# Two placements in a fused attention and feed-forward kernel: the scale of the second weight, and the planes of the last head pair of batch 0

## The chip, the cores and the metric

The kernel runs on one core of one Trainium2 chip. The metric is the time of one execution in device microseconds (us); of several runs the median is given. A change of more than 0.3% (about 3.1 us) is what a measurement of this kernel can tell from no change.

## What is computed

Eight batches of eight heads attend over 512 local tokens and 32 global ones (head size 64). A global query sees all 544 keys, a local query the global keys and the local keys within 32 positions. The result, 4352 rows of 512, goes through a feed-forward block.

```python
s_ll = np.where(np.abs(pos[:, None] - pos[None, :]) <= 32, s_ll, -1e9)
a_l = sm(np.concatenate([s_lg, s_ll], axis=-1))          # softmax
out_l = np.matmul(a_l, np.concatenate([v_g, v_l], axis=2))
x = attn_out.transpose(0, 2, 1, 3).reshape(B * S, H * D)
h = x @ w_in                                             # 512 -> 2048
g = h * np.cos(h)
return g @ w_out                                         # 2048 -> 512
```

## The kernel before

All matmuls are done in fp16 with each operand held as a high plane and a low plane (value minus high), so each product is three matmuls. Planes need scales, powers of two taken from the largest absolute value.

**Weights.** `w_in` and `w_out` come as raw 64-bit words. For `w_out`, `w_out_max` (L401) loads each of 16 row blocks and reduces it to its largest value; `w_out_done` (L428) joins the 16 results, spreads the maximum over the partitions with one matmul into a PSUM tile `pm_wo` (`spread_max`, L183), reads it back and makes the scale `wsc`. Only then can `w_out_piece` (L418) decode the 16 blocks. For each, ACT scales the words (`y_wo`, L237), DVE makes the low bits (L263, L266, which need no scale) and joins them (L268), ACT rounds to the high plane (L281) and POOL subtracts for the low plane (L231, two instructions). Blocks 8 to 15 are loaded again into a ring of two buffers (L244), so that a load waits until an earlier block is decoded.

**Attention.** It goes by pairs of heads, four pairs to a batch. For each pair come scores (L606, L607), row minima (L623), exponentials (L446), probability planes in four query tiles (`sc_d`, L672), their transposes (`sc_e`, L707), the product with v (`av_a`, `acc`, L729) and the planes `xh`, `xl` of the feed-forward's input (`av_b`, L766). In batch 0 the transposes are done by TensorE: eight of 128x128 into one PSUM tile `tr`, copied to `pt` by DVE for tiles 0 and 2 and by ACT for tiles 1 and 3 (L715). The table `PLS` says for batch 0 how each tile of each pair makes its planes:

- 1: per head, ACT writes the high plane straight from the exponentials (L702), DVE the low plane (L705)
- 2: per head, DVE writes the high plane (L704), DVE the low plane (L705)
- 3 and 4: the exponentials are normalized in place by POOL (3, L685) or ACT (4, L688); ACT rounds (L693), POOL subtracts per head (L695)

**Feed-forward.** A chunk is 256 tokens. `m1_a` (L908) makes the first product into PSUM tiles `ph`, `m1_b` to `m1_d` the cosine, `m2_a` (L975 to L977) the second product, which needs the decoded blocks of `w_out`.

**The order.** Work is written into numbered slots, and in a slot into phases (PA0 first, PJ last); walking through slots and phases gives the program's order. Tiles of one tag share buffers, and in the program's order each new tile waits for a buffer that an earlier one gives back. The tag `ph` has three PSUM buffers, for `tr`, for `acc` of the last two pairs of batch 0, for `pm_wo` and for the `ph` tiles. A second number, the priority, says which ready instruction an engine's order takes first; `at(slot, phase, f, ..., pr=(slot, phase))` sets it apart from the place in the program, and without `pr` both are the same. A planner then fixes each engine's queue, and on the chip each queue runs in that order.

Pair p of batch 0 starts at slot u = -21 + p; its planes are in slot u + 5, its transposes in slot u + 6 (phase PA2), its `acc` in slot u + 7. So the transposes of pair 2 stand in slot -13 and those of pair 3 in slot -12. The first two `ph` tiles are opened in slot -5; `w_out_done` stands in slot -4, phase PJ.

Of the kernel before, what the change touches and what calls it, by code (L numbers as in the profile page):

```python
# [65 lines left out]
GFB = 3  # L66
GFW = 3
UW = 1
PLS = [[3, 4, 3, 4], [3, 4, 3, 4], [3, 4, 3, 4], [1, 2, 1, 4]]
DEFN = [0, 0]  # L70
TPE = [1, 1, 1, 1]
TPV = [1, 0, 1, 0]
# [37 lines left out]
WO = -13  # L110
WOS = 2
WOL = -5
WOD = -4
GWM = 0
U1 = 2
SP1 = 2
# [21 lines left out]
def body(tc, qk, v, wi, wo, mask, out):  # L138
# [5 lines left out]
    with ExitStack() as ctx:  # L144
# [527 lines left out]
        def sc_d(b, p, i):  # L672
# [3 lines left out]
            w = WIN[i][1]  # L676
            pl = PLS[p][i] if b == 0 else (PL0, PL1, PL)[min(b, 2)]
            if b < 2 and DEFN[b]:
# [327 lines left out]
        def at(slot, phase, f, *a, pr=None):  # L1006
            e = (phase, len(ev[slot]), f, a)
            ev[slot].append(e)
            pr = (slot, phase) if pr is None else pr if isinstance(pr, tuple) else (pr, phase)
            rank[slot, e[1]] = pr + (slot, e[1])  # L1010
# [75 lines left out]
                at(WE + k, PJ, w_in_load, k + 4, pr=W0 + k)  # L1086
        at(WE + 7, PA, w_in_done, pr=(W0 + 7 - WM, PH2))
        for k in range(16):
            at(WO + k // WOS, PI, w_out_max, k)
        for k in range(8):  # L1090
            at(WOL, PJ, w_out_load, k)
        at(WOD, PJ, w_out_done)
        for k in range(16):
            at(k // 2 + PO, WOPH, w_out_piece, k)
        at(LV1, PJ, load_v, 1)
# [113 lines left out]
```

## Time and profile before

| | |
|---|---|
| median of 3 runs (lowest to highest) | 1033.6 us (1032.02 to 1034.86) |
| the profiled execution: its own time | 1034.44 us |
| its span in the trace | 1032.6 us |
| busy: PE, ACT, DVE, POOL | 87%, 70%, 69%, 45% of the span |
| mean granted TensorE clock | 0.954 |

The span runs from the first to the last recorded instruction; the execution's own time holds 1.8 us more. Busy shares are means over the whole span, and the stages differ: up to about 245 us the weights are prepared and batches 0 and 1 go through attention, after that the steady loop over chunks runs.

### The profile page before, as it was taken

The numbers are of one execution on the slowest core, as the hardware profiler recorded it, in microseconds if no ns is written. First come the engines' busy times: TensorE is split into PE (matmuls) and PEld (weight loads), VectorE is DVE, ScalarE is ACT, GpSimd is POOL, SyncE is SP. The second block draws the span as 40 slices with busy tenths as digits, with TensorE's granted clock in tenths as the row PEclk, the third lists the DMA queues.
The fourth block names the chain that finished last, engine by engine and source line by source line (L and its number), as shares of the span: only waits on it lengthen the run. The fifth ranks groups of instructions, "written<-read, shape, count | busy, mean of one in ns | idle before, by whom it ended". The sixth has DMA issues, their size and how long they took to land.

```text
span 1032.6 us, 21117 instructions
## 1 busy us (share of the span) xinstructions
PE 893.3 (87%) x7947; PEld 609.2 (59%) x7947; DVE 710.7 (69%) x1811; ACT 717.9 (70%) x1468; POOL 461.8 (45%) x494
## 2 busy tenths in 40 slices
PE   1245878769999999899899999999989999999996
PEld 0134645444666766666666666666666667766663
DVE  4999786897477777867777777868777766433231
ACT  5788798785577776877687768777777876544342
POOL 3696477984233333333334324343333343534442
PEclk9996979788999999999999999999989999999998
DMA  9796145775254464454645354545536452100000
GB/s 361 269 303 246 15 142 142 181 164 139 70 103 111 103 157 108 99 115 97 147 93 119 91 145 93 122 91 153 111 81 109 107 88 61 34 21 22 1 21 21
DMA packets 165822, 120.19 MB, mean 116 GB/s; under 512 B 143064, under 2 KB 143064, under 8 KB 163672
## 3 DMA queue, kind: packets, MB, share of 16 engines
q1 hardware_dynamic: 165720, 118.85, 46.3%
q8 instruction: 62, 1.02, 0.4%
q14 instruction: 40, 0.33, 0.1%
HBM read 56.00 MB, written 8.91 MB: 63 GB/s over the span
## 4 chain that ended last, share of the span: by engine, by line
PE 33%; DVE 28%; ACT 15%; DMA 11%; POOL 5%; issue 5%; SPq 1%; ACTq 0%; DVEq 0%; POOLq 0%
PE ph L919 13%; DMA qkr<-qk 7%; PE po L975 5%; PE po L976 5%; PE po L977 5%; DVE planes L705 4%; DVE t L623 4%; DVE u L942 3%; ACT L446 3%; ACT planes L702 3%; ACT t L446 3%; DMA vr<-v 2%; DVE kl L538 2%; POOL w L954 2%; DVE qm L497 2%
## 5 line engine op out<-in xcount | busy, mean ns | idle before, releaser
L919 PE MATMUL ph<-xh,wi_h 128*128 128x256 f16 x1024 | 281.9, 276 | 10.0 <-DVE gf L956 9.8
L919 PE MATMUL ph<-xl,wi_h 128*128 128x256 f16 x1024 | 282.1, 275 | 0.0
L919 PE MATMUL ph<-xh,wi_l 128*128 128x256 f16 x1024 | 282.0, 275 | 0.0
L961 POOL TENSOR_TENSOR gl<-gf,gh 128x512 f16<-128x512 f32 x136 | 167.2, 1233 | 236.5 <-ACT gh L960 236.5
L954 POOL TENSOR_TENSOR w<-w 128x512 f32<-128x512 f32 x136 | 141.5, 1044 | 266.0 <-ACT w L446 266.0
L919 PEld LDWEIGHTS <-wi_h 128*128 128x128 f16 x2176 | 211.8, 99 | 52.3 <-issue 12.4
L975 PE MATMUL po<-wo_h,gh 128*128 128x512 f16 x544 | 206.5, 384 | 28.2 <-DVE o L983 17.1
L976 PE MATMUL po<-wo_l,gh 128*128 128x512 f16 x544 | 209.6, 385 | 10.6 <-POOL wo_l L231 10.6
L977 PE MATMUL po<-wo_h,gl 128*128 128x512 f16 x544 | 209.5, 386 | 0.0
L446 ACT ACTIVATE w<-u,ca 128x512 f32<-128x512 f32 x136 | 97.8, 721 | 109.9 <-DVE u L942 109.3
L942 DVE SCALAR_TENSOR_TENSOR u<-u,cm,ph 128x512 f32<-128x512 f32 x136 | 100.9, 742 | 97.3 <-ACT u L941 97.3
L446 ACT ACTIVATE t<-t,mn 128x192 f32<-128x192 f32 (+1 forms) x256 | 116.9, 458 | 49.3 <-DVE mn L623 48.9
L956 DVE SCALAR_TENSOR_TENSOR gf<-w,ph 128x512 f32<-128x512 f32 x136 | 92.6, 682 | 58.3 <-POOL w L954 58.1
L960 ACT CAST gh<-gf 128x512 f16<-128x512 f32 x136 | 83.1, 611 | 69.8 <-DVE gf L956 59.2
L919 PEld LDWEIGHTS <-wi_l 128*128 128x128 f16 x1088 | 107.5, 99 | 15.1 <-issue 1.4
L623 DVE CUSTOM_DVE_ANT_0 t<-ps,msk,al 128x192 f32<-128x192 f32 (+1 forms) x256 | 99.5, 426 | 11.7 <-PE ps L607 11.2
L941 ACT ACTIVATE u<-ph,cm 128x512 f32<-128x512 f32 x136 | 92.1, 678 | 21.4 <-PE ph L919 19.5
L977 PEld LDWEIGHTS <-gl 128*128 128x128 f16 x544 | 53.8, 99 | 75.5 <-issue 13.9
L705 DVE SCALAR_TENSOR_TENSOR planes<-t,sm,planes 128x224 f16<-128x224 f32 (+1 forms) x198 | 88.6, 496 | 10.7 <-ACT planes L702 10.7
L976 PEld LDWEIGHTS <-gh 128*128 128x128 f16 x544 | 53.7, 99 | 70.7 <-issue 22.7
L975 PEld LDWEIGHTS <-gh 128*128 128x128 f16 x544 | 53.1, 98 | 62.8 <-issue 14.5
L702 ACT ACTIVATE planes<-t,sm 128x192 f16<-128x192 f32 (+1 forms) x196 | 74.3, 453 | 0.0
(185 smaller groups left out, 1427.7 us busy)
## 6 DMA issues: line engine op xcount, KB each, us to landing
qkr<-qk SPq DMA_DIRECT2D x29, 608.0 KB, 4.8
vr<-v SPq DMA_DIRECT2D x8, 1280.0 KB, 7.7
kh<-qa SPq DMA_DIRECT2D x62, 152.0 KB, 2.6
out<-o SPq DMA_DIRECT2D x34, 256.0 KB, 2.7
raw_wm<-wo SPq DMA_DIRECT2D x16, 512.0 KB, 7.6
qa<-kl SPq DMA_DIRECT2D x31, 152.0 KB, 3.9
kl<-kl SPq DMA_DIRECT2D x31, 152.0 KB, 4.6
wo_h<-wi SPq DMA_DIRECT2D x4, 1024.0 KB, 6.7
```

The source lines that it names most:

```text
L446: ins = nc.scalar.activation(*a, **k).ins
L623: nc.vector.tensor_tensor_reduce(t[:, h], pt[:, h], msk[:, MOFF[i] : MOFF[i] + w], al, 3.0e38, ALU.add, ALU.min, mn[:, h : h + 1],)
L702: nc.scalar.activation(hi, t[:, h], AF.Identity, scale=r)
L705: nc.vector.scalar_tensor_tensor(lo, t[:, h], r, hi, op0=ALU.mult, op1=ALU.subtract)
L919: nc.tensor.matmul(ph[:, a], w[:, kc, f], x[:, kc, q], start=first and ip == 0, stop=last and ip == 2, skip_group_check=True,)
L942: nc.vector.scalar_tensor_tensor(u, u, m, ph, op0=ALU.subtract, op1=ALU.subtract)
L954: nc.gpsimd.tensor_tensor(w, w, w, op=ALU.mult)
L956: nc.vector.scalar_tensor_tensor(gf, w, 0.5, st.pop(("ph", c, j)).rearrange("p a b -> p (a b)"), op0=ALU.subtract, op1=ALU.mult,)
L961: nc.gpsimd.tensor_tensor(gl, gf, gh, op=ALU.subtract)
L975: nc.tensor.matmul(po[k], gh[:, q], wo_h[:, f], start=(f == 0), stop=False)
L976: nc.tensor.matmul(po[k], gh[:, q], wo_l[:, f], start=False, stop=False)
L977: nc.tensor.matmul(po[k], gl[:, q], wo_h[:, f], start=False, stop=(f == NJ - 1))
```

## The change

```diff
-PLS = [[3, 4, 3, 4], [3, 4, 3, 4], [3, 4, 3, 4], [1, 2, 1, 4]]
+PLS = [[3, 4, 3, 4], [3, 4, 3, 4], [3, 4, 3, 4], [1, 1, 1, 1]]
...
-WOD = -4
+WOE = -20
...
         for k in range(16):
-            at(WO + k // WOS, PI, w_out_max, k)
+            at(WOE + k // WOS, PJ, w_out_max, k, pr=(WO + k // WOS, PI))
...
-        at(WOD, PJ, w_out_done)
+        at(WOE + 7, PJ, w_out_done, pr=(WO + 7, PI))
```

With `WO = -13` and `WOS = 2` the 16 maxima keep their priorities (slots -13 to -6, phase PI) but stand in the program in slots -20 to -13. `w_out_done` stands in slot -13, phase PJ, instead of slot -4, phase PJ; its priority goes from slot -4, phase PJ, to slot -6, phase PI. Separately, tiles 1 and 3 of pair 3 of batch 0 make their planes in way 1 instead of ways 2 and 4.

## Rows read from the trace of the kernel before

**Rows 1.** The page: the shares of the chain that ended last.

```profile
PE 33%; DVE 28%; ACT 15%; DMA 11%; POOL 5%; issue 5%; SPq 1%; ACTq 0%; DVEq 0%; POOLq 0%
```

**Rows 2.** Windows: us; busy time (instructions) by engine; clock, DMA share, GB/s.

```profile
98.20:104.80 6.60, 4.66 (x66) 3.84 (x63) 5.98 (x18) 6.60 (x15) 0.00 (x0) 0.79 0.00 1
104.80:112.40 7.60, 6.97 (x138) 5.83 (x139) 2.12 (x8) 3.16 (x7) 1.06 (x2) 1.00 0.02 4
112.40:245.00 132.60, 99.40 (x898) 66.27 (x896) 109.54 (x278) 113.48 (x228) 101.58 (x135) 0.81 0.58 136
245.00:1032.60 787.60, 749.16 (x6583) 510.17 (x6581) 509.36 (x1270) 522.57 (x1075) 291.87 (x257) 0.98 0.41 91
```

**Rows 3.** Timeline of DVE: start, duration, operation; in brackets its wait and releaser.

```profile
96.10 0.68 DVE L288 TENSOR_REDUCE wos<-raw_wm 128x1 f32<-128x512 f32 x1
...
97.95 0.29 DVE L186 TENSOR_SCALAR d_wo<-ident,wm_o 128x128 bf16<-128x128 f32 x1
...
111.68 0.28 DVE L190 TENSOR_REDUCE r_wo<-pm_wo 128x1 f32<-128x128 f32 x1
```

**Rows 4.** Timeline of PE, 98 to 112 us.

```profile
98.68 0.42 PE L750 MATMUL acc<-pt,vh 128*64 128x128 f16 x4
...
101.09 1.17 PE L714 MATMUL tr<-ident,planes 128*128 128x128 f16 x16
...
111.36 0.23 PE L188 MATMUL pm_wo<-d_wo,ones 128*128 128x128 bf16 x1
```

**Rows 5.** Timeline of ACT, 100 to 113 us.

```profile
100.07 1.55 ACT L702 ACTIVATE planes<-t,sm 128x192 f16<-128x192 f32 x4
101.51 0.79 ACT L688 ACTIVATE t<-t,sm 128x192 f32<-128x192 f32 x2
...
104.31 0.52 ACT L693 CAST planes<-t 128x384 f16<-128x384 f32 x1
107.94 1.01 ACT L715 COPY pt<-tr 128x1024 f16<-128x1024 f16 x1 [3.12 <-PE tr L714]
...
110.96 0.74 ACT L561 ACTIVATE vh<-vr 128x640 bf16<-128x640 f32 x1 [0.63 <-PE gacc L855]
...
112.42 0.75 ACT L237 ACTIVATE y_wo<-wo_h,wsc 128x512 f32<-128x512 f32 x1
```

**Rows 6.** Timeline of DVE at the last pair of batch 0.

```profile
99.83 0.58 DVE L704 TENSOR_SCALAR planes<-t,sm 128x224 f16<-128x224 f32 x2
...
101.18 1.45 DVE L705 SCALAR_TENSOR_TENSOR planes<-t,sm,planes 128x192 f16<-128x192 f32 x4
...
110.37 0.75 DVE L776 SCALAR_TENSOR_TENSOR xl<-acc,xs,xh 128x512 f16<-128x512 f32 x1 [5.08 <-ACT xh L775]
```

**Rows 7.** Timeline of POOL, 100 to 117 us.

```profile
104.96 1.06 POOL L695 TENSOR_TENSOR planes<-t,planes 128x192 f16<-128x192 f32 x2 [7.43 <-ACT planes L693]
114.99 1.75 POOL L231 TENSOR_TENSOR wo_l<-y_wo,wo_h 128x256 f16<-128x256 f32 x2 [8.98 <-ACT wo_h L281]
```

**Rows 8.** Waits of PE, 112 to 245 us: total us, times, longest.

```profile
PE po L975 <- ACT wo_h L281: 11.1, 5, 5.3
PE po L976 <- POOL wo_l L231: 10.6, 4, 5.2
```

**Rows 9.** Timeline: one DVE operation alone and beside POOL, and POOL then.

```profile
83.17 0.45 DVE L266 TENSOR_SCALAR lo_wo<-wo_h 128x512 uint16<-128x512 uint16 x1
...
127.26 1.28 DVE L266 TENSOR_SCALAR lo_wo<-wo_h 128x512 uint16<-128x512 uint16 x1
```

**Rows 10.** Timeline of POOL at 127 us.

```profile
127.00 1.22 POOL L954 TENSOR_TENSOR w<-w 128x512 f32<-128x512 f32 x1
```

**Rows 11.** Waits of the SyncE queue, 95 to 245 us.

```profile
SPq L244 <- DVE lo_wo L266: 2.2, 2, 1.9
```

**Rows 12.** Timeline of the SyncE queue: first and last of six loads.

```profile
165.83 0.57 SPq L244 DMA_DIRECT2D raw_wo<-wo  x1
...
214.06 0.34 SPq L244 DMA_DIRECT2D raw_wo<-wo  x1
```

## The prediction

> **What bounds the kernel now.** I read the page first, then windows by stage, then each engine's timeline around the edit, then the waits behind it. The chain that ended last is shared out: PE has a third, DVE and ACT together more [rows 1]. The windows say where. From 245 us on PE is busy for 749.2 of 787.6 us, so what happens there is PE's own work, which the edit leaves alone. From 112.4 to 245 us no engine is full, but ACT has 113.5 of 132.6 us, DVE 109.5, POOL 101.6 and PE only 99.4 [rows 2]: three engines that hand work to each other in fixed queues, with PE waiting at the end. In this stretch PE waits 11.1 us for high planes and 10.6 us for low planes of w_out [rows 8]; so the decoding of w_out is one of the things that pace it.
>
> Before it lies a hole. Between 104.8 and 112.4 us ACT is busy for 3.16 of 7.60 us, DVE for 2.12, POOL for 1.06; just ahead of it, from 98.2 to 104.8, ACT is busy throughout [rows 2]. Two things make the hole, and the edit touches both.
>
> The first is the scale of w_out. Its last maximum is taken at 96.10 and the operand of the spreading matmul, d_wo, is finished at 97.95 + 0.29 = 98.24 [rows 3]. But that matmul runs at 111.36 [rows 4], 13.1 us later, and the first decoding by ACT at 112.42 [rows 5]. What it waits for is a buffer: in the program pm_wo follows acc of pair 3 and two ph tiles, and with three buffers it gets the one that acc of pair 3 gives back. That is read for the last time by xl, at 110.37 + 0.75 = 111.12 [rows 6], a quarter of a microsecond before the matmul.
>
> The second is tile 3 of pair 3. ACT normalizes it at 101.51, rounds it at 104.31 [rows 5], POOL subtracts from 104.96 to 106.02 [rows 7], and ACT, which stood idle for 3.12 us, copies the transposes at 107.94 [rows 5]. Then come the rest of acc, xh and xl.
>
> **The change part by part.** *Instructions of the planes.* Tile 3 loses two ACT scalings (0.79 us), one ACT rounding (0.52 us) [rows 5] and two POOL subtractions (1.06 us) [rows 7]; tile 1 loses two DVE multiplications (0.58 us) [rows 6]. ACT gets four more high planes; four take 1.55 us [rows 5]. DVE gets two more low planes at 1.45 / 4 = 0.36 us, 0.7 us [rows 6]. Net: ACT 1.55 - 1.31 = +0.2 us, DVE +0.1 us, POOL -1.06 us. The sums are small; the path is what moves. ACT would write all eight high planes from 100.07 to about 103.2 (twice 1.55 us). DVE follows within half a microsecond, so tile 3 is ready for its transposes at about 103.7, not 106.02. ACT then still has to do what it now does between 102.3 and 104.3, the planes of the global rows, xh of pair 2 and the copy of tile 1, some 2 us, and can copy tile 3 at about 105.3 in place of 107.94. I take 2.6 us for this step, the lower bound being nothing (if the copy still waits for DVE) and the upper 3.12 us, ACT's whole wait there.
>
> *The place of the scale.* pm_wo now stands behind the four tr tiles of pair 2 and ahead of acc of pair 2 and of pair 3's transposes. A buffer of pair 2's is free at about the time d_wo is ready: acc of pair 2 begins at 98.68 [rows 4], which needs the first of those tiles copied. The matmul (0.23 us) could run at 98.3 to 98.7, the reading (0.28 us) and some six tiny DVE instructions after it put wsc at about 100. The moved maxima keep their priorities and their loads wait for the same things, so I let them cost nothing, and nothing passes them on SyncE's queue that did not before. The cover is DVE: it is full until 104.8 [rows 2] and the tiny instructions now stand there; without cover they cost about 1 us.
>
> What does the early scale buy? ACT's queue is full until about 105.3 with work of higher priority, so the decoding begins there and not at 100. After the 2.6 us have been taken out of the hole of 7.60 - 3.16 = 4.44 us, 4.44 - 2.6 = 1.8 us remain in which ACT waits, for acc and for the global product (0.63 us of it is such a wait [rows 5]). Decoding fills it: two blocks need two scalings (0.75 us each, one of them in [rows 5]) and two roundings. I take 1.7 us after the 0.2 us of added ACT work, less 0.1 us for gaps that stay. Lower bound nothing. For the upper bound the decoding alone paces the next stretch; it starts at 105.3 in place of 112.42, which is worth 7.1 us.
>
> *What is late next.* With x complete at about 108.5, the product of the global rows, the transposes of the second global group and batch 1's v planes, whose buffers come free behind it [rows 5], move with it. The stretch to 245 us has ACT at 86%, and I carry the gain through it unchanged; from 245 us on PE is the bound and the gain is only shifted.
>
> Sum: 2.6 + 1.5 = 4.1 us earlier. The profiled execution took 1034.44 us (span 1032.6), 0.8 us above the median of 1033.6, so 1030.3 for such an execution and **1029.5 us** as a median, 0.40% less. No change is what a measurement shows within 0.3%, 3.1 us: 1030.5 to 1036.7.
>
> **A rule weighed.** The same DVE instruction on w_out's words took 0.45 us at 83.17 and 1.28 us at 127.26 [rows 9], while POOL ran from 127.00 to 128.22 [rows 10]. So a DVE instruction can be held up by POOL. [...] It is rival D below.
>
> **The rivals.**
>
> *A, the forecast:* both parts of the hole shrink and the gain lasts. 1027.5 to 1031.5 us.
>
> *B, nothing lasts.* The hole closes, but the stretch to 245 us is paced by something that does not begin earlier. For it: no engine is full there, so waits and not work set its length. Against it: its first ACT work waits for the product that ends batch 0 [rows 5]. At most 1 us stays: 1032.6 us.
>
> *C, decoding paces the stretch.* For it: PE's 21.7 us of waits for w_out [rows 8]. Against it: the blocks have a low priority and share three engines with batch 1. The gain is 7.1 us: 1026.5 us.
>
> *D, POOL holds up DVE.* Each of the eight low planes waits for one subtraction of w_out, 1.75 / 2 = 0.88 us [rows 7], 7.0 us in all against a gain of 4.1: 1036.5 us. Against it: the subtraction of a block needs ACT's scaling and rounding, which stand behind pair 3's high planes in ACT's queue; POOL was idle from 98.2 to 104.8 us [rows 2]. I expect one meeting or none.
>
> *E, slower: the transposes stand behind the scale.* PE's queue is in order, and pm_wo is now in front of acc of pair 2 and of pair 3's transposes (101.09 [rows 4]). If d_wo comes late, both wait. From 98.68 on acc of pair 2 moves with it, from 101.1 on pair 3 too; the change turns slower by more than 0.3% when pm_wo runs later than about 101.1 + 4.1 + 3.1 = 108.3. This needs the last maximum, taken at 96.10, to be put behind pair 3's planes in DVE's queue. Against it: the priorities up to there are as before. At 110 us it gives about 1038 us.
>
> *F, slower: loads of w_out hold SyncE's queue.* Six loads of later blocks stand there (165.83 to 214.06 [rows 12]), each waiting for DVE to free one of two buffers, with batch 1's copies and transposes behind them. Now they wait 2.2 us together, 1.9 at the longest [rows 11]. If a new order made each wait 1.9 us, 6 x 1.9 - 2.2 = 9.2 us more against 4.1: 1038.7 us. It decides from about 1.6 us each (9.4 us in all, which is 2.2 + 4.1 + 3.1). For it: any edit here gives the planner a new order for all that follows.
>
> **How the numbers follow.** A 0.50, B 0.13, C 0.14, D 0.08, E 0.05, F 0.10. Of A about 0.40 lies below 1030.5 us and 0.10 above. Faster: 0.40 + 0.14 = 0.54. Same: 0.10 + 0.13 + 0.08 = 0.31, of which 0.02 of D runs over its bound: 0.29. Slower: 0.05 + 0.10 + 0.02 = 0.17. The likeliest case alone: 1027.5 to 1031.5 us. The range for 8 in 10 takes in B, most of C and D: 1024.5 to 1036.5 us, which leaves E, F and the best of C outside.
>
> **What would show it.** In the changed kernel's trace: pm_wo on PE before 100 us, ahead of pair 3's transposes; no POOL subtraction for pair 3; ACT's copy of tile 3 near 105.3 and xl of pair 3 ended near 108.5 us; y_wo starting between 100 and 107 us; fewer than 21.7 us of PE's waits for w_out; PE becoming full near 241 us in place of 245. It would be wrong if x is complete early and PE still fills up at 245 us (B), if pm_wo runs after 101 us (E), or if the low planes of pair 3 take twice their 0.36 us (D).

## The result and the profile after

The changed kernel takes 1020.32 us (median of 4 runs, 1017.62 to 1022.88), the kernel before 1032.81 (1031.79 to 1034.86). The ratio is 0.9869, with a 95% interval from 0.9838 to 0.9901: 1.3% faster. Forecast were 1029.5 us and a range that ended at 1024.5. The sign was right, the size was not: about 13 us against 4.1.

The page of the changed kernel: busy time by engine, and the shares of the chain that ended last, which answer to [rows 1].

```profile
span 1016.1 us, 21123 instructions
...
PE 880.3 (87%) x7947; PEld 603.6 (59%) x7947; DVE 712.2 (70%) x1811; ACT 718.5 (71%) x1469; POOL 461.4 (45%) x492
...
PE 29%; DVE 29%; DMA 16%; ACT 14%; issue 7%; POOL 4%; SPq 1%; ACTq 0%; DVEq 0%; POOLq 0%
```

Windows of the changed kernel, columns as in [rows 2]; the first line is the whole span.

```profile
0.00:1016.10 1016.10, 880.34 (x7947) 603.63 (x7947) 712.24 (x1811) 718.45 (x1469) 461.42 (x492) 0.97 0.47 118
98.20:104.80 6.60, 3.67 (x60) 2.62 (x60) 6.03 (x23) 6.60 (x15) 0.00 (x0) 0.98 0.00 1
104.80:112.40 7.60, 6.92 (x70) 4.92 (x71) 6.32 (x11) 6.01 (x10) 4.03 (x6) 0.57 0.01 2
112.40:245.00 132.60, 109.01 (x1083) 74.62 (x1079) 107.60 (x272) 114.26 (x230) 103.83 (x136) 0.95 0.56 136
245.00:1016.10 771.10, 727.40 (x6473) 498.25 (x6470) 507.89 (x1266) 518.82 (x1068) 286.27 (x253) 0.99 0.41 93
```

The hole is filled: from 104.8 to 112.4 us ACT is busy for 6.01 us where it had 3.16, DVE for 6.32 where it had 2.12. But the large difference is in the third stage. PE is busy for 109.01 us there where it had 99.40 [rows 2], and its granted clock is 0.95 in place of 0.81. What is left for the last stage is 6473 matmuls and not 6583, so that 110 more are done by 245 us.

The span fell by 16.5 us. PE does the same 7947 matmuls in both kernels; its busy time fell from 893.3 to 880.3 us, and what is left of the span from 139.3 to 135.8. So in these two executions 12.9 us are the same matmuls taking less time, and 3.6 us are less waiting. But the clock of before's profiled execution, 0.954, is as low as that of any of the 92 runs of that kernel beside the experiments. Their mean is 0.965, that of the changed kernel's four runs 0.973. By these means the clock's share is (0.973 - 0.965) / 0.97 x 885 = 7 us, an estimate: about half of the gain.

Now the steps. PE's timeline of the changed kernel, 97 to 112 us, against [rows 4]:

```profile
97.46 0.23 PE L188 MATMUL pm_wo<-d_wo,ones 128*128 128x128 bf16 x1
...
100.19 1.69 PE L714 MATMUL tr<-ident,planes 128*128 128x128 f16 x16
103.26 0.61 PE L714 MATMUL tr<-ident,planes 128*128 128x128 f16 x8 [1.38 <-DVE pt L715]
105.48 1.01 PE L714 MATMUL tr<-ident,planes 128*128 128x128 f16 x8 [1.62 <-DVE pt L715]
...
108.00 0.39 PE L919 MATMUL ph<-xh,wi_h 128*128 128x256 f16 x1
...
110.32 0.42 PE L919 MATMUL ph<-xh,wi_l 128*128 128x256 f16 x1
110.67 0.53 PE L750 MATMUL acc<-pt,vh 128*64 128x192 f16 x4
```

The last of these, the product of pair 3's tile 3, in the kernel before:

```profile
109.00 0.36 PE L750 MATMUL acc<-pt,vh 128*64 128x192 f16 x4 [0.55 <-ACT pt L715]
```

DVE's timeline, against [rows 3, 6]:

```profile
97.12 0.29 DVE L186 TENSOR_SCALAR d_wo<-ident,wm_o 128x128 bf16<-128x128 f32 x1
...
98.05 0.28 DVE L190 TENSOR_REDUCE r_wo<-pm_wo 128x1 f32<-128x128 f32 x1
...
113.69 0.75 DVE L776 SCALAR_TENSOR_TENSOR xl<-acc,xs,xh 128x512 f16<-128x512 f32 x1
```

ACT's timeline, against [rows 5]:

```profile
99.49 2.99 ACT L702 ACTIVATE planes<-t,sm 128x192 f16<-128x192 f32 x8
...
103.02 0.76 ACT L237 ACTIVATE y_wo<-wo_h,wsc 128x512 f32<-128x512 f32 x1
...
106.53 1.01 ACT L715 COPY pt<-tr 128x1024 f16<-128x1024 f16 x1
...
108.95 0.76 ACT L237 ACTIVATE y_wo<-wo_h,wsc 128x512 f32<-128x512 f32 x1 [0.72 <-POOL wo_l L231]
110.39 0.77 ACT L237 ACTIVATE y_wo<-wo_l,wsc 128x512 f32<-128x512 f32 x1 [0.68 <-POOL wo_l L231]
...
112.23 0.67 ACT L775 ACTIVATE xh<-acc,xs 128x512 f16<-128x512 f32 x1
```

POOL's first work after 98 us, against [rows 7]:

```profile
106.98 3.37 POOL L231 TENSOR_TENSOR wo_l<-y_wo,wo_h 128x256 f16<-128x256 f32 x4 [10.30 <-ACT wo_h L281]
```

The matmul of the scale runs 0.05 us after d_wo is finished (97.12 + 0.29 = 97.41), 13.9 us earlier than before, and decoding begins at 103.02 in place of 112.42. But x of batch 0 is complete *later*: xl of pair 3 ends at 113.69 + 0.75 = 114.44, not at 111.12. ACT's copy of tile 3 did move forward, to 106.53 from 107.94, although PE's transposes of pair 3 waited 1.38 and 1.62 us for DVE's copies. The loss comes behind this copy. Before, it ended at 108.95 and the product of tile 3 followed at 109.00. Now it ends at 107.54, and the product runs at 110.67: twelve matmuls of ph, 108.00 to 110.7, stand ahead of it in PE's queue, and the clock is 0.57 from 104.8 to 112.4 us. Then xh on ACT stands behind a scaling of w_out (112.23, where acc is finished at 111.56), the third of three, two of which waited for POOL. On DVE xl stands behind a joining of w_out (113.08). The part that the forecast gave 2.6 us went the wrong way, and the kernel still won three times the forecast.

Waits of PE, 112 to 245 us, of the changed kernel; in [rows 8] the first two were for w_out, 21.7 us together.

```profile
PE pm_qk L479 <- DVE d_qk L473: 8.5, 5, 2.7
PE pm_v L479 <- DVE d_v L473: 5.2, 1, 5.2
PE ph L919 <- DVE gf L956: 4.6, 4, 1.8
PE po L976 <- POOL wo_l L231: 2.1, 2, 1.1
```

The waits for w_out are down to 2.1 us. One of the second product's three groups of matmuls in the same stretch (mean ns of one behind the comma; the last figure is the idle time ahead of it), first of the kernel before, then of the changed one:

```profile
L976 PE MATMUL po<-wo_l,gh 128*128 128x512 f16 x31 | 14.2, 457 | 10.6 <-POOL wo_l L231 10.6
```

```profile
L976 PE MATMUL po<-wo_l,gh 128*128 128x512 f16 x56 | 21.2, 379 | 2.1 <-POOL wo_l L231 2.1
```

Before, 93 matmuls of the second product (31, 30 and 32) were done by 245 us, and the rest of chunks 0 and 1 was still to come; now it is 168, each at 0.38 and not 0.46 us. Chunk 0's first output leaves at 220.05 us in place of 247.13, chunk 1's at 255.10 in place of 274.83.

When the decoding runs is seen from ACT's scalings: shortest/median/longest ns, first and last start. Blocks 0 to 7 are scaled in their own tiles (`wo_h`, `wo_l`), later ones from `raw_wo`. First before, then after:

```profile
L237 ACT ACTIVATE y_wo<-wo_h,wsc x4: 747/756/762, 112.4 to 137.0; 128x512 f32<-128x512 f32 x4
L237 ACT ACTIVATE y_wo<-wo_l,wsc x4: 757/766/772, 113.1 to 150.1; 128x512 f32<-128x512 f32 x4
```

```profile
L237 ACT ACTIVATE y_wo<-wo_h,wsc x4: 756/759/762, 103.0 to 117.4; 128x512 f32<-128x512 f32 x4
L237 ACT ACTIVATE y_wo<-wo_l,wsc x4: 747/762/773, 103.7 to 120.2; 128x512 f32<-128x512 f32 x4
```

The first scaling is 9.4 us earlier, the eighth 30 us. Before batch 1's q and k planes begin on ACT at about 129 us, blocks pass at some 3 us each (103.0 to 124.7 for nine); after that at some 10 us each, because they share ACT, DVE and POOL with batch 1. Before the change five blocks and a sixth at 127.17 went ahead of that point, after it nine.

### The profile page after: what moved, and what is told of

Read it like the earlier page. It is cut to its first block, busy times and chain, and to the rows that moved or that the text cites. A ratio compares the mean times of both kernels' runs of the same rounds, so it can differ in the third digit from the quotient of the medians.

```text
span 1016.1 us, 21123 instructions
## 1 busy us (share of the span) xinstructions
PE 880.3 (87%) x7947; PEld 603.6 (59%) x7947; DVE 712.2 (70%) x1811; ACT 718.5 (71%) x1469; POOL 461.4 (45%) x492
## 4 chain that ended last, share of the span: by engine, by line
PE 29%; DVE 29%; DMA 16%; ACT 14%; issue 7%; POOL 4%; SPq 1%; ACTq 0%; DVEq 0%; POOLq 0%
PE ph L919 12%; DMA qkr<-qk 9%; PE po L975 5%; PE po L977 5%; PE po L976 5%; DVE planes L705 5%; DVE t L623 4%; DMA vr<-v 4%; ACT planes L702 3%; DVE u L942 3%; DVE kl L538 3%; ACT L446 3%; DVE qm L497 2%; ACT t L446 2%; POOL w L954 2%
## 5 line engine op out<-in xcount | busy, mean ns | idle before, releaser
L976 PE MATMUL po<-wo_l,gh 128*128 128x512 f16 x544 | 207.1, 381 | 2.1 <-POOL wo_l L231 2.1
L977 PE MATMUL po<-wo_h,gl 128*128 128x512 f16 x544 | 206.1, 380 | 0.3 <-POOL gl L961 0.3
L919 PEld LDWEIGHTS <-wi_l 128*128 128x128 f16 x1088 | 107.3, 99 | 14.6 <-issue 1.2
L705 DVE SCALAR_TENSOR_TENSOR planes<-t,sm,planes 128x192 f16<-128x192 f32 (+1 forms) x200 | 87.7, 487 | 10.8 <-ACT planes L702 10.8
L976 PEld LDWEIGHTS <-gh 128*128 128x128 f16 x544 | 53.3, 98 | 69.3 <-issue 20.8
```

The source lines that it names most:

```text
L705: nc.vector.scalar_tensor_tensor(lo, t[:, h], r, hi, op0=ALU.mult, op1=ALU.subtract)
L919: nc.tensor.matmul(ph[:, a], w[:, kc, f], x[:, kc, q], start=first and ip == 0, stop=last and ip == 2, skip_group_check=True,)
L976: nc.tensor.matmul(po[k], gh[:, q], wo_l[:, f], start=False, stop=False)
L977: nc.tensor.matmul(po[k], gl[:, q], wo_h[:, f], start=False, stop=(f == NJ - 1))
```

## The experiments

Ratios are to the kernel before, with 95% intervals. "PE's idle time" is 132.60 us less PE's busy time in the window 112.4:245: 33.2 us before, 23.6 after.

**Which part, and through what.** E1 keeps the early scale and puts the planes back:

```diff
 (changed kernel)
-PLS = [..., [1, 1, 1, 1]]
+PLS = [..., [1, 2, 1, 4]]
```

> The new place of the scale alone, with the old planes of the last pair. If the early scale is the cause (the decoding of w_out runs ahead and PE no longer waits for it), nearly the whole gain stays: 0.985 to 0.992 of the kernel before, pm_wo on PE before 100 us, PE's waits for w_out up to 245 us under 5 us. If the planes of the last pair carry a good part of it, as the prediction had it (2.6 of 4.1 us), at most a third stays: about 0.996.

Measured: 1017.01 us, 0.9829 (0.9778 to 0.9879). pm_wo at 97.69, the eighth block scaled at 119.5, PE's idle time 22.9 us. This is a little more than the range foresaw; the interval reaches into it.

E2 is the other half, the kernel before with the new planes:

```diff
 (kernel before)
-PLS = [..., [1, 2, 1, 4]]
+PLS = [..., [1, 1, 1, 1]]
```

> The new planes of the last pair alone, with the scale at its old place. By the prediction's first step 2.6 us less, 0.9975, and xl of pair 3 ended near 108.5 us. If the gain is the scale's, no change a measurement can tell: 0.997 to 1.003, with PE's waits for w_out near the 21.7 us of before.

Measured: 1030.12 us, 0.9973 (0.9944 to 1.0002). DVE's timeline and PE's waits:

```profile
108.61 0.75 DVE L776 SCALAR_TENSOR_TENSOR xl<-acc,xs,xh 128x512 f16<-128x512 f32 x1 [3.48 <-ACT xh L775]
```

```profile
PE pm_qk L479 <- DVE d_qk L473: 8.4, 3, 4.9
PE po L975 <- ACT wo_h L281: 5.5, 4, 2.9
```

Alone, the planes do most of what the forecast said of them: xl ends at 109.36, 1.8 us earlier where 2.6 were forecast, and pm_wo moves with it to 109.60. PE's idle time stays at 33.2 us.

E3 leaves the program's order as it was before and gives the scale's matmul a buffer of another tag:

```diff
 (kernel before, spread_max)
-pm = ps.tile([P, P], F32, tag="ph", name=f"pm_{name}")
+pm = ps.tile([P, P], F32, tag="po" if name == "wo" else "ph",
+             name=f"pm_{name}", bufs=2 if name == "wo" else 3)
```

> The kernel before with the old place and the old planes; only the PSUM tile of the scale takes a buffer of another tag, which is free since pair 1. If it was the wait for a buffer that held the scale, pm_wo runs before 100 us and the gain is that of the new place alone, 0.985 to 0.992. If the place in the program or its priority matters for itself, the time stays within 0.3% of before.

Measured: 1019.71 us, 0.9845 (0.9804 to 0.9887). PE's timeline:

```profile
98.48 0.23 PE L189 MATMUL pm_wo<-d_wo,ones 128*128 128x128 bf16 x1
```

Nothing but the buffer is changed, and the matmul moves from 111.36 to 98.48 and the whole gain appears, though xl of pair 3 ends at 116.53, later still than in the changed kernel. So what held the matmul was the wait for a PSUM buffer, and this wait was the price.

E17 and E18 run E1 and the changed kernel again, side by side on one chip.

> The new place of the scale with the old planes once more, beside the changed kernel on the same chip. By the prediction's first step the planes give 2.6 us on top of the scale: this is 0.25% slower than the changed kernel. If the decoding takes ACT ahead of pair 3's x anyway, the planes give nothing there: within 0.3% of the changed kernel.

> The changed kernel itself, for the two runs beside it: 0.984 to 0.990 of the kernel before, as measured.

Measured: E17 1023.08 us, 0.985 (0.9824 to 0.9876); E18 1023.96 us, 0.9867 (0.9836 to 0.9899). Once the scale is early, the planes add nothing that these runs can tell.

**Is it PE's waits for w_out?** E4 lets the second product of chunks 0 and 1 read planes of w_in, which are ready long before, so that PE never waits for the decoding:

```diff
 (kernel before, m2_a; wh and wl take the place of wo_h[:, f] and wo_l[:, f])
+if c < 2:
+    n = slice(f // 4 * DM, f // 4 * DM + DM)
+    wh, wl = wi_h[:, f % 4, n], wi_l[:, f % 4, n]
+else:
+    wh, wl = wo_h[:, f], wo_l[:, f]
```

> The kernel before, where the second product of chunks 0 and 1 takes its weights from the planes of w_in, ready long before, in place of those of w_out: same shapes and count, but no wait for the decoding (this part of the result is not the reference's). If PE's wait for the decoding is what the change takes away, this gains as much as the change without moving the scale: 0.980 to 0.990. If the gain comes from a new order of batch 1's work or from ACT's filled hole, under 0.4%: 0.996 to 1.000.

Measured: 1028.43 us, 0.9934 (0.991 to 0.9958). PE's waits, 112 to 245 us:

```profile
PE ph L919 <- DVE gf L956: 11.1, 3, 4.3
PE pm_qk L479 <- DVE d_qk L473: 10.3, 2, 7.7
```

The time lies between the two forecasts. With 21.7 us of waits taken away, 21.4 us of others stand there, for the feed-forward's cosine (`gf`) and for batch 1's scales (`d_qk`); before, these two were 6.4 us. They are work of the same DVE, ACT and POOL that decode.

E5 is the same edit on the changed kernel:

> The changed kernel, where the second product of chunks 0 and 1 takes its weights from the planes of w_in (this part of the result is not the reference's). If the change has already taken away PE's wait for the decoding (2.1 us of it are left), this adds next to nothing: 0.983 to 0.990 of the kernel before. If the waits still paced the stretch, another 0.6%, as the same edit gave in the kernel before: 0.980.

Measured: 1021.3 us, 0.9897 (0.9869 to 0.9926): nothing on top of the change.

E7 takes away work, not only the wait: E4's edit, and blocks 2 to 5 are not decoded, block 0 standing for them later.

```diff
 (E4)
-    at(k // 2 + PO, WOPH, w_out_piece, k)
+    if k not in (2, 3, 4, 5):
+        at(k // 2 + PO, WOPH, w_out_piece, k)
```

> The kernel before with no wait of chunks 0 and 1 for the decoding, and with the decoding of blocks 2 to 5 left out altogether (the second product takes block 0 in their place; the result is not the reference's). It takes from the stretch up to 245 us what the change moves into the hole ahead of it: some 5.4 us of ACT, 6 of DVE and 5.5 of POOL. If the rest of the gain, beyond PE's waits, is this work out of the stretch, the two together give the whole gain: 0.982 to 0.988. If not, it stays near 0.993.

Measured: 1009.67 us, 0.9791 (0.9768 to 0.9814), PE's idle time 17.9 us: a larger gain than either forecast. Against E4 the four blocks are worth (0.9934 - 0.9791) x 1033 = 14.8 us. What PE waits for by name matters less than how much decoding the three engines do beside batch 1.

**Decoding against the last pair's x.** In E6 every scaling of w_out follows xh of pair 3 on ACT, so x comes first; in E8 it follows the second `u` of chunk 0.

```diff
 (changed kernel, decoding; E8 has st["u_ins", 0, 1])
+if s is wsc:
+    tc.add_manual_dep(ins, st["xh_ins", 0, 3].name, order, ...)
```

> The changed kernel with ACT's first scaling of w_out's words put behind xh of pair 3 in ACT's order; the scale itself stays early. The head start of the decoding is gone (it begins near 107 us instead of 103), and pair 3 has ACT to itself, so that xl ends near 108.5 us instead of 114.4. If the hours of the decoding are what pays, a part of the gain is lost: 0.988 to 0.995. If an early x pays as much, as the prediction had it, nothing is lost or a little won: 0.983 to 0.988.

> As the run before last, but the first scaling stands behind the second u of chunk 0 in ACT's order, so that the decoding begins some 113 us into the run, as before the change, although the scale is there at 99. If the early decoding is the cause, the gain is gone: 0.994 to 1.003. If it is the freed PSUM buffer or the new place in the program, it stays near 0.987.

Measured: E6 1030.65 us, 0.9984 (0.9963 to 1.0005), with xl ended at 109.95 us, 4.5 us earlier than in the changed kernel and 1.2 earlier than before, and PE's idle time at 32.3 us. E8 1037.5 us, 1.0048 (1.0026 to 1.0069), scaling from 115.5 us on, idle time 34.4 us. E6 and E8 both lie above their ranges. An early scale that isn't used early brings nothing that can be told, although in E6 x is complete earlier.

E12 lets two blocks go first and holds the others behind xh of pair 3:

```diff
 (E6)
-if s is wsc:
+if s is wsc and st["n_wo"] > 2:
```

> The changed kernel, where only the scalings of blocks 2 and later stand behind xh of pair 3 in ACT's order; blocks 0 and 1 keep their head start at 103 us. xl of pair 3 then ends near 110 us instead of 114.4, and block 2 starts a microsecond later. If the late x still costs something in the changed kernel, this beats it: 0.980 to 0.985. If only the hours of the decoding count, as the kernel held behind x suggests, it is no faster: 0.986 to 0.992.

Measured: 1032.74 us, 0.9979 (0.9954 to 1.0004); xl ended at 112.04, the seventh block was scaled at 121.6, idle time 33.2 us. This was to combine both advantages, and has neither; no range held it.

**How many blocks ahead of batch 1.** E13 holds blocks from the eighth on behind ACT's first `qa` of batch 1, E14 from the sixth on; in E16 that `qa` follows the tenth block. `n_wo` counts the scalings.

```diff
 (changed kernel; E14 has > 5)
+if s is wsc and st["n_wo"] > 7:
+    tc.add_manual_dep(ins, st["qa_ins", 1, 0].name, order, ...)
```

```diff
 (changed kernel, E16)
+if s is wsc and st["n_wo"] == 10:
+    tc.add_manual_dep(st["qa_ins", 1, 0], ins.name, order, ...)
```

> The changed kernel; only the scaling of block 7 and all later ones stands behind the first qa of batch 1 (129 us) in ACT's order, so that seven blocks are scaled ahead of batch 1's work and not nine. Scale, place, pair 3's x (ended at 114 us) and the first u (118 us) stay as in the changed kernel. If the number of blocks decoded ahead of batch 1's work sets the gain, most of it is gone: 0.993 to 1.000. If the gain comes from the late x and u, that is from the order of chunk 0 against batch 1, it stays: 0.985 to 0.990.

> As the run before, with five blocks ahead, the number of the kernel before. If the number of blocks sets the gain, nothing is left: 0.996 to 1.006. If the order of chunk 0 does, 0.985 to 0.990.

> The changed kernel, where ACT's first qa of batch 1 stands behind the scaling of block 9, the tenth, so that ten blocks are scaled ahead of batch 1's work and not nine; it is the last one whose words are loaded by then. From five to seven to nine blocks the time fell by some 0.5% for two, so one more is worth some 2.5 us: 0.982 to 0.986. If batch 1, which now starts about 1.5 us later, is what binds in the changed kernel, no gain: 0.986 to 0.992.

Measured: E14 1031.19 us, 0.997 (0.9948 to 0.9991); E13 1026.01 us, 0.9917 (0.9896 to 0.9937), between its two ranges; the changed kernel with its nine has 0.9869; E16 1028.43 us, 0.9906 (0.9872 to 0.994). Over these kernels, from five to nine blocks, each is worth (0.997 - 0.9869) / 4 x 1033 = 2.6 us; the tenth brings nothing, and `qa` starts at 133.80 there, 4.5 us later than in the changed kernel. In E14 the scale is early, its first two blocks are scaled from 103.54 on, and most of the gain is gone: most of it lies in the blocks that pass ahead of batch 1.

The count alone does not order all runs. By the trace the kernel before scales six blocks ahead of that `qa` (127.17 against 128.83), not five as E14's text has it, and is at 1.000; E6 and E12 have seven, as E13 has, and 0.998. Three more blocks at 2.6 us are 7.8 us of a gain of about 13.

E15 asks the same from the other side: the kernel before, its late scale and its waits, with blocks 2 to 5 not decoded.

> The kernel before with the decoding of blocks 2 to 5 left out (the second product takes block 0 in their place in every chunk; the result is not the reference's); it still waits for the other blocks, scale and x are as late as before, and chunk 0's first u stands at 113 us. The blocks that count for the second product then come some four earlier, as in the changed kernel. If the decoding ahead of batch 1 is the cause, this gives at least the gain of the change: 0.978 to 0.988. If the order of chunk 0 against batch 1 is, little: 0.992 to 1.000.

Measured: 1021.52 us, 0.9875 (0.9854 to 0.9895): as much as the change, without any part of it. Idle time 24.7 us.

E11 moves the decoding in the changed kernel four slots forward, `PO` from 1 to -3. These `at` have no `pr`, so the place in the program moves with the priority:

> The changed kernel with the decoding of w_out four slots higher in priority. If the hours of the decoding set the gain, its last block is scaled before 193 us and PE idles less than 23.6 us between 112 and 245 us: 0.980 to 0.986. If what is left of PE's idling comes from batch 1's own chain (it waits 13.7 us for batch 1's scales), pushing it back by the decoding makes it no faster: 0.986 to 0.993.

Measured: 1025.92 us, 0.9919 (0.9894 to 0.9943). The nine blocks are scaled within 0.4 us of the changed kernel's times and the last one at 197.1 us, not before 193, so the edit brought no block forward. But PE waits 10.5 us for `gf` in place of 4.6, and its idle time is 28.6 us. The block count doesn't explain this run.

**Does idling cost PE its clock?** E9 and E10 add 128 matmuls that nobody reads, eight behind each `m2_a` of chunks 0 and 1, to the kernel before and to the changed one:

```diff
+if c < 2:
+    fl = ps.tile([P, CT], F32, tag="att", name=f"fl_{c}_{j}")
+    for n in range(8):
+        nc.tensor.matmul(fl, wi_h[:, n % 4, :P], st["x", 0][0][:, n % 4, :CT],
+                         start=True, stop=True)
```

> The kernel before with eight more matmuls of 256 columns (their result is read by nobody) behind each of the 16 second-product groups of chunks 0 and 1: 128 matmuls, some 14 us of PE at the full clock, in the stretch from 112 to 260 us where PE now idles and its granted clock falls to 0.81. If a good part of the change's gain is matmuls that run at the higher clock, because PE idles less, this work pays for itself or better: clock in the stretch above 0.86, time 0.990 to 1.003. If the clock plays no part and only PE's waits count, the added work costs what does not fit into the waits: 1.004 to 1.014.

> The same 128 matmuls in the changed kernel, where the granted clock in the stretch is 0.95 already. There is little clock left to win, so by either theory it is slower than the changed kernel: 0.992 to 1.002 of the kernel before, against 0.987. If the clock is part of the cause, the loss here is larger than in the kernel before.

Measured: E9 1032.51 us, 0.9981 (0.9961 to 1.0001); E10 1023.67 us, 0.9889 (0.9841 to 0.9938). Windows of E9:

```profile
0.00:1031.00 1031.00, 896.82 (x8075) 617.05 (x8075) 714.20 (x1811) 718.28 (x1468) 462.86 (x494) 0.97 0.47 117
...
112.40:245.00 132.60, 109.32 (x954) 74.49 (x949) 107.27 (x260) 109.57 (x215) 106.45 (x138) 0.91 0.55 132
```

The whole span of E10:

```profile
0.00:1022.00 1022.00, 893.50 (x8075) 616.52 (x8075) 713.31 (x1811) 718.48 (x1469) 462.94 (x492) 0.97 0.47 118
```

The added matmuls take 18.8 us of PE in E9 (window 112:275) and the kernel is no slower. PE's busy time is 896.8 us; without the added ones it is 878, up to 15 us less than the 893.3 of the kernel before, and the clock of the stretch is 0.91 in place of 0.81. The rest of the span, in which PE isn't busy, is 134.2 us, where it was 139.3. So part of the added work fits into waits, and part seems to be paid for by faster matmuls around it. How much is uncertain: the profiled execution of the kernel before has the lowest clock of its 92 runs, and by the mean clocks, 0.965 before and 0.974 in E9's ten runs, some (0.974 - 0.965) / 0.97 x 885 = 8 us of the 15 are left, an estimate. The planner's order moved too.

E10 answers against its text, which had it slower by either theory: with 19.4 us of added matmuls it can't be told from the changed kernel. Its mean clock over four runs, 0.973, is the same as the changed kernel's. PE is not busy for 128.5 us of its span, where it was 135.8. So added work was free where there was no clock to win as well, and the two runs don't show how much the clock is worth.

**All together.** Over the 18 profiled kernels without added matmuls (the one before among them), PE's idle time in the window 112.4:245 goes from 17.9 (E7) to 34.4 us (E8) and the time follows it: a straight line through them has 1.47 us of time for each microsecond of idling, with a correlation of 0.97. E11 and E12, which the count of blocks misses, are near this line: with 28.6 and 33.2 us of idling it gives 0.993 and 1.000, and they have 0.9919 and 0.9979. The slope is above 1, and the granted clock in this window differs too: 0.81 in the kernel before (33.2 us of idling) and 0.83 in E8 (34.4), against 0.95 in the changed kernel (23.6) and 0.91 in E7 (17.9). That the clock makes the slope was not shown. The line is a correlation; the idle time is itself a result of the order. E9 and E10 show its limit: with 23.3 and 18.0 us of idling the line gives 0.986 and 0.978, and they have 0.9981 and 0.9889. Idle time filled with work that isn't needed gains nothing.

## Why the prediction was wrong in size

**Right.** That the scale's matmul waited for the buffer which xl of pair 3 gives back, and would run as soon as d_wo is ready (98.3 to 98.7 forecast, 97.46 found; E3 shows the cause). Decoding between 100 and 107 us. No subtraction by POOL for pair 3. Less than 21.7 us of waits for w_out.

**The term that failed: 1.5 us for the early scale.** It was priced at the microseconds in which ACT stood idle (1.8 us were left of the hole; the step's sentence ends with 1.7, the sum takes 1.5). E1, E3 and E17 measure the early scale by itself at 16.8, 14.1 and 14.6 us. A block decoded in the hole doesn't save the ACT time that it fills there. It saves its place in the stretch behind, where a block takes some 10 us to pass and takes time of three engines from batch 1 and the feed-forward. E13 and E14 give 2.6 us of the whole for each block moved, and E15 3.3 us for each left out ((1034.69 - 1021.52) / 4). The upper bound of 7.1 us failed with it: it counted how much earlier the decoding starts. The first block came 9.4 us earlier, but the eighth 30 us.

**The other term: 2.6 us for pair 3.** Alone it is 1.8 us in the trace and at most 0.6% in time (E2), about as forecast. In the changed kernel the copy of tile 3 came 1.4 us earlier, but xl 3.3 us later, since the decoding came in between on ACT and DVE and matmuls of ph on PE, whose queue the step didn't look at; and E6 shows that it didn't matter, x being 4.5 us earlier there without a gain. The forecast let both terms add up in one hole. They competed for the same engines, and the one that lost was the one worth little.

**"I carry the gain through it unchanged".** The stretch didn't shift, it was compressed: 110 more matmuls were done by 245 us. What it left out is that PE's own time there isn't fixed: one matmul of the second product took 0.38 in place of 0.46 us, and by the mean clocks of the runs about 7 us of the gain, an estimate, are the same matmuls at a higher granted clock. "From 245 us on the gain is only shifted" nearly held: there one matmul of L976 takes 0.381 us in both kernels (195.8 us for 514, 185.8 us for 488).

**The rivals.** C, decoding paces the stretch, named the right stage and the right waits, with half the size. E4 shows why the named waits were not the whole price: without their 21.7 us the kernel gains 0.66%, as PE waits for other work of the same engines. B's condition came true in part (x early and no gain, E6), without B's result. D wasn't seen: of the low planes of pair 3 seven take 2.61 us in a row, 0.37 us apart, and POOL's first subtraction begins at 106.98, behind them. Neither trace has a low plane of pair 3 beside a subtraction of w_out, so the 0.88 us that D gave each is not shown. What D feared shows a little later, on a joining of w_out by DVE (L268): 1.16 us at 109.75, while POOL subtracts until 110.35, and 0.69 us at 113.08 with POOL idle. E and F weren't seen.

**Left open.** Why E6 and E12 with seven blocks ahead have 0.998 and E13 with seven 0.992, why the kernel before with six is no faster than E14 with five, and why E11 loses 0.5% at the same decoding times. E12 and E11 wait longer for `gf`, 12.8 and 10.5 us; which instruction of which queue starts that wasn't tried. That the early decoding makes the gain is shown (E3, E6, E8, E14); how it adds up to the whole 13 us is shown only in part. How much of the gain is the clock and how much the waiting is known from means of runs and not from an experiment that changes the clock alone. Of the kernels that compute the whole reference, E1, E3 and E17 are as fast as the changed one within their intervals, and none is shown to be faster.

## What to carry to other kernels

A tiny instruction can hold a whole chain of work when its place in the program ties it to a shared buffer (here a matmul of 0.23 us, at 111.36 us and with a buffer of its own at 98.48): look for small operations that run long after their input is ready, and give them another place or another buffer. Price work that is moved into a hole by what it took where it stood, in the crowded stretch, and not by the idle time that it fills. And where TensorE idles in a mixed stage, look whether its matmuls there are slower as well; here one took 0.46 us and then 0.38.

## What the runs showed of the hardware

The clock that TensorE was granted differed between stretches and between the two kernels, and this was no small thing. PE's timeline of the kernel before, at 121 us:

```profile
120.48 0.28 PE L919 MATMUL ph<-xh,wi_h 128*128 128x256 f16 x1 [2.49 <-DVE gf L956]
...
121.03 0.27 PE L919 MATMUL ph<-xh,wi_l 128*128 128x256 f16 x1
121.14 0.27 PE L919 MATMUL ph<-xh,wi_h 128*128 128x256 f16 x1
...
121.72 0.42 PE L919 MATMUL ph<-xl,wi_h 128*128 128x256 f16 x1
121.93 0.42 PE L919 MATMUL ph<-xh,wi_l 128*128 128x256 f16 x1
```

PE had waited 2.49 us for DVE. Matmuls of the same shape then start every 0.11 us, at a granted clock of 1.00 (window 120.4:121.3), and half a microsecond later every 0.21 us, at 0.50 (window 121.5:122.3), though PE is busy throughout. In the windows from 112.4 to 245 us the clock was 0.81 where PE was busy for 75% and 0.95 where it was busy for 82%. The busy share of the same stretch does not tell it alone: from 104.8 to 112.4 us PE was busy for 92% before and 91% after, and the clock was 1.00 and 0.57; in the changed kernel the waits of 1.38 and 1.62 us had come just before. What set the clock these runs don't show. That 128 useless matmuls, 18.8 and 19.4 us of PE, cost nothing measurable in either kernel was expected of the kernel before by one of two theories, and of the changed kernel by none.
